# Layer two's third row block in halves of 256, and another order of the work list, in a two-layer transformer kernel

## The chip, the cores and the metric

The kernel runs on one core of a Trainium2 chip. The metric is the device time of one execution in microseconds (us). The profile is that of one further execution, taken by the hardware profiler; its span, from the first to the last instruction, is 1654.3 us.

## What is computed

An input x of 2048 rows and 512 columns (bf16) goes through attention, a two-product MLP, and both again with the same weights. Attention has 32 heads of width 16.

```python
def _A_ref(x, wqkv, wo):
    qkv = (x @ wqkv).reshape(B, S, 3, H, Dh).transpose(2, 0, 3, 1, 4)
    q, k, v = qkv[0], qkv[1], qkv[2]
    scores = jnp.einsum("bhqd,bhkd->bhqk", q, k) * (Dh ** -0.5)
    p = _softmax(scores, axis=-1)
    o = jnp.einsum("bhqk,bhkd->bhqd", p, v)
    return o.transpose(0, 2, 1, 3).reshape(B, S, D) @ wo
def _B_ref(x, w1, w2):          # w1 is 512 x 1792, w2 is 1792 x 512
    return jnp.maximum(x @ w1, 0) @ w2
x = x + _A_ref(_layernorm(x), wqkv, wo)
x = x + _B_ref(_layernorm(x), w1, w2)
x = x + _A_ref(_layernorm(x), wqkv, wo)
x = x + _B_ref(_layernorm(x), w1, w2)
```

## The kernel before

**Row blocks.** The queries of each layer are worked off in chunks (`chunks`, L440): (layer, number) gives the first tile of 128 rows and the number of tiles. Layer one has four chunks of 512 rows. Layer two has three of 512 and two of 256, the last 512 rows in halves.

**The loop.** A planner in Python writes one long program (the `while units:` loop, L1140 and on, to L1280 or so). Its unit is a score block: one head, 128 keys, 512 queries (or two key blocks of 256 queries in a half). Each turn of the loop banks three units in one of two PSUM tiles ps_s (score matmuls of TensorE, L1240, four heads lying in four groups of 32 rows of the array), and ScalarE takes the exponential of all three, or of two (L1249, 1536 or 1024 columns). Where it is two, VectorE computes the third block's exponential in bit arithmetic (lin L970, step L1010, cube L1018 to L1022). TensorE then multiplies the exponentials by the values into ps_o (L876). When a segment (four heads, all keys) is through, the sums are copied to u (L800, or L798 with an earlier part added), the denominators go by DMA to c and back (SP queue, L805 and L825), are spread over 32 partitions by a DMA of POOL's queue (L827) or by a shuffle on VectorE (L837), and multiplied into ot (L813). There are three buffers u, c and r. TensorE may repeat a score matmul where it would be idle.

**The work list.** Everything else is done beside this: q, k and v, the output product with wo and its addition to x (`o_group`, L630), the norm and its transposes (`ln_rows`, `ln_groups`, L550), the first MLP product with its relu (`h_group`, L664; w1 is fetched tile by tile through four buffers, L644) and the second (`z_group`, L690, with the store of the rows in layer two, L693). They stand in a list `work`. Each turn of the loop takes from it, from the front, the first group whose inputs the plan has as ready, as far as a pace allows that is set by what is left and how many turns remain. When all heads of a chunk are through, `rest_of_chunk` gives that chunk's groups, which are added at the end of the list. `before(l, j)` names the earlier chunk whose use of the shared tiles xn2T and ht has to be over.

**The end.** After the last exponential, `run_all` works off what the list still holds, with relus on ScalarE (L662). Then the last 256 rows follow in an order written out by hand: output product (L1303, with `add`), norm, MLP. Into this the second MLP products of the two tiles before (1536 to 1791) are woven: tile one under the norm (`half_part(0, ...)`), tile two one product a step in the MLP loop (`half_part(1, [ft])`).

Of the kernel before, what the change touches and what calls it, by code (L numbers as in the profile page):

```python
# [24 lines left out]
def kernel(  # L25
# [199 lines left out]

    slot = [0]
    now_pe = [0.0]
    now_dve = [0.0]  # L230
    mode = [None]
# [206 lines left out]


    chunks = {(l, j): (j * TPC, TPC) for l in range(2) for j in range(NQS)}  # L440
    chunks[1, NQS - 1] = (NKB - TPC, TPC // 2)
    chunks[1, NQS] = (NKB - TPC // 2, TPC // 2)

    def columns(l, j):

# [72 lines left out]
    def ln_rows(tag, tt, n, i):  # L518

        if tag not in ln_seq:  # L520
            ln_seq.append(tag)
        at_tag = ln_seq.index(tag)
        prev = ln_seq[at_tag - 1]
        old = [("xn", ln_seq[at_tag - 2], k) for k in range(TPC)] if at_tag > 1 else []
        if ("st", tag, i) not in made:
            task(830, lambda: ln_stats(tag, tt + i, i), [("st", tag, i)], old)
        if i == n - 1:

            def rstd():
                ln_rstd(tag, 0)  # L530
                ln_newton(tag)
                mark(("rs", tag, 3), lag=RSTD_LAG)

            task(500, rstd, [("rs", tag, 3)], each(n, "st", tag) + old)
            for k in range(n):
                task(
                    325, lambda k=k: ln_apply(tag, tt + k, k), [("xn", tag, k)],
                    [("xT", prev, k), ("rs", tag, 3)],
                )

    def ln_groups(tag, dst, at_column, n, war):
# [83 lines left out]
    def o_group(l, j, i):  # L625
        tt, n = chunks[l, j]
        a = columns(l, j)[1] + i * P

        def fin(b):
            nc.vector.tensor_add(out=x_t[tt + i][:], in0=x_t[tt + i][:], in1=b)  # L630
            mark(("o", l, j, i))
            ln_rows(("ln2", l, j), tt, n, i)

        return mm_group(
            [(ot[t][:, a : a + P], wo[:, t // 2, :]) for t in range(NT)], fin,
            [("o", l, j, i)],
            [("ot", l, j, t, i) for t in range(NT)],
        )
# [64 lines left out]
    def before(l, j):  # L703

        if (l, j) == (0, 0):
            return None
        return (l, min(j, NQS - 1) - 1) if j else (0, NQS - 1)

    def rest_of_chunk(l, j):

        b = before(l, j)
        xj, a, w = columns(l, j)
        n = w // P
        war_h = each(chunks[b][1], "z", *b) if b else []
        war_x = each(NF, "h", *b) if b else []
        gs = [o_group(l, j, i) for i in range(n)]
        gs += ln_groups(("ln2", l, j), xn2T, a, n, war_x)
        gs += [h_group(l, j, ft, war_h) for ft in range(0, NF, QS // w)]
        if (l, j) != (1, NQS - 1):
            gs += [z_group(l, j, i) for i in range(n)]  # L720
        if l == 0:
            gs += ln_groups(("ln1", 1, j), xnT[j], 0, TPC, [])
            gs.append(k_group(1, 0, j))
            gs += [v_group(1, kb) for kb in range(j * TPC, (j + 1) * TPC)]
            gs += [k_group(1, T, j) for T in range(1, 4)]
        return gs
# [20 lines left out]
    for l in range(2):  # L747


        if l == 0:  # L750
            steps = [(0, range(4), 0, TPC), (0, range(MID), TPC, 2 * TPC)]
            steps += [(0, range(MID), 2 * TPC, NKB), (0, range(MID, 4), TPC, NKB)]
            steps += [(j, range(4), 0, NKB) for j in range(1, NQS)]
        else:
            steps = [(0, range(4), 0, NKB - TPC), (1, range(NEXT), 0, NKB - TPC)]
            steps += [(0, range(4), NKB - TPC, NKB), (1, range(NEXT, 4), 0, NKB)]
            steps += [(1, range(NEXT), NKB - TPC, NKB)]
            steps += [(j, range(4), 0, NKB) for j in range(2, NQS + 1)]
        for j, Ts, a, b in steps:
            for T in Ts:  # L760
                sums = acc[8 * j :] if l else acc0
                add_run(l, j, T, range(a, b), load=a and sums, store=b < NKB and sums)
# [7 lines left out]
    def finish_segment(sg, last):  # L770
        l, j, t, e = sg["l"], sg["j"], sg["t"], sg["e"]
        sums_wait[0] += 1
        if sg["store"] is not None:

            def store():
                if sg["load"] is not None:
                    nc.vector.tensor_add(out=sg["store"], in0=sg["load"], in1=ps_o[:])
                else:
                    nc.vector.tensor_copy(out=sg["store"], in_=ps_o[:])
                mark(("po",))  # L780
                sums_wait[0] -= 1

            musts.append((EVAC, now_pe[0] + PE_TO_DVE, store))
            return
        n = norm_no[0]
        norm_no[0] += 1
        if n >= NU:
            run_until(("m", n - NU))
        u, r, c = ubuf[n % NU], rbuf[n % NU], cbuf[n % NU]
        lane = DH if e == 0 else DH - 1  # L790
        width = sg["w"]
        at_column = columns(l, j)[1]
        sums = u[lane : P : 32, 0:width]
        c = c[:, 0 : width // 32]

        def copy():
            if sg["load"] is not None:
                nc.vector.tensor_add(out=u[:], in0=sg["load"], in1=ps_o[:])  # L798
            else:
                nc.vector.tensor_copy(out=u[:, 0:width], in_=ps_o[:, 0:width])  # L800
            mark(("po",))
            mark(("u", n))
            sums_wait[0] -= 1
            if sg not in segs[-2:]:
                nc.sync.dma_start(out=c, in_=sums)  # L805
                mark(("c", n), lag=C_LAG)

        musts.append((77 + 1.045 * width, now_pe[0] + PE_TO_DVE, copy))
        b = before(l, j)
        war = each(chunks[b][1], "o", *b) if b else []  # L810

        def mul(a, w):
            nc.vector.scalar_tensor_tensor(  # L813
                out=ot[t][:, at_column + a : at_column + a + w], in0=u[:, a : a + w], scalar=mask[e][:, 0:1],
                in1=r[:, a : a + w], op0=ALU.mult, op1=ALU.mult,
            )
            for i in range(a // P, (a + w) // P):
                mark(("ot", l, j, t, i))

        ended[l, j] = ended.get((l, j), 0) + 1  # L820
        quick = sg["load"] is not None or ended[l, j] == NT

        def recip():
            nc.vector.reciprocal(out=c, in_=c)
            nc.sync.dma_start(out=sums, in_=c)  # L825
            if not quick:
                nc.gpsimd.dma_start(  # L827
                    out=r[:, 0:width],
                    in_=bass.AP(
                        tensor=sums.tensor, offset=sums.offset,  # L830
                        ap=[list(sums.ap[0]), [0, 32], [1, width]],
                    ),
                )
            mark(("r", n), lag=U_LAG if quick else R_LAG)

        def spread():
            nc.vector.stream_shuffle(  # L837
                out=r[:, 0:width], in_=u[:, 0:width], mask=[lane] * 32
            )

        def spread_mul():
            if quick:
                spread()
            mul(0, width)

        def direct(i):
            if i == 0:
                spread()
            a = i * P
            nc.vector.reciprocal(out=r[:, a : a + P], in_=r[:, a : a + P])  # L850
            mul(a, P)

        def direct_all():
            for i in range(width // P):
                direct(i)

        ots = each(width // P, "ot", l, j, t)
        if last:
            last_steps.append(direct)
        elif sg is segs[-2]:  # L860
            task(3100, direct_all, ots + [("m", n)], war + [("u", n)])
        else:
            task(165, recip, [("r", n)], [("c", n)], place=0)
            cost = 105 + 1.1 * width + (200 + 1.05 * width if quick else 0)
            task(cost, spread_mul, ots + [("m", n)], [("r", n)] + war)
        if ended[l, j] == NT and not last:
            work.extend(rest_of_chunk(l, j))

    pend = deque()
    musts = []  # L870
# [269 lines left out]
    while units:  # L1140
# [67 lines left out]
        if first["l"] and first["early"]:  # L1208
            rest = sum(x[0][0]["early"] for x in itertools.islice(units, 400)) / W - 20.0
        pace = (  # L1210
            3.0 if first["short"] and not first["l"] else max(todo / max(rest + (0.0 if first["j"] == NQS - 1 and not first["l"] else AHEAD[first["l"]] if first["j"] < NQS - 1 else -6.0), 6.0), 0.5)
        )
        owed[0] = min(owed[0] + pace, 6.0) if todo else 0.0
        hurry[0] = pace > (
# [67 lines left out]
    run_all()  # L1282
    ending[0], wide[0] = False, True
    users.clear()
    l, j = 1, NQS
    tag = ("ln2", l, j)
    tt, n_rows = chunks[l, j]
    rows = range(n_rows)
# [58 lines left out]
    for ft in range(NF + 1):  # L1347
# [17 lines left out]
        if ft:  # L1365
            for i in rows:
# [1 line left out]
                    banks[i], ht[ft - 1][:, part(i)], w2[:, ft - 1, :],  # L1368
                    False, ft == NF, "h",
                )  # L1370
        if ft < NF:
            half_part(1, [ft])
    for i in rows:
        copy = nc.vector.tensor_copy if i % 2 else nc.scalar.copy
        uses(copy(out=x_t[tt + i][:], in_=at_bank(banks[i])), banks[i])
# [33 lines left out]
```

The softmax here doesn't subtract the row's maximum and nothing guards it: scores larger than these inputs give would overflow.

## Time and profile before

| | |
|---|---|
| three executions | 1643.58, 1649.41, 1651.98 us; median 1649.41 |
| the profiled execution | 1656.09 us, span 1654.3 us |
| busy: TensorE, VectorE, ScalarE | 1509.3, 1507.4, 1590.0 us |
| mean granted TensorE clock | 0.981 |
| exponentials on ScalarE | 749 of 1536 columns at 1593 ns, 616 of 1024 at 1166 ns, one of 512 |
| score matmuls (L1240) | 4396 of 512 columns, 1164 of 256 |
| w1 tiles fetched (L644 and at the start) | 126 of 128 KB |

How to read it: PE is TensorE's matmuls, PEld its weight loads, DVE is VectorE, ACT is ScalarE, POOL is GpSimd, SPq the queue that issues DMAs. A row of the page's groups names line, engine, operation, output and inputs, then busy time, mean length in ns, and the idle time of the engine ahead of these instructions with what ended it. Idle time counts where the engine is the one that everything waits for. Matmuls that lie in different row groups of the array overlap, so their lengths don't add up to time.

### The profile page before, as it was taken

The page shows a single profiled execution, that of the slowest core. Times are in us where ns is not written, and L with a number is a line of the kernel's source. Part 1 is how long each engine was busy: PE and PEld are TensorE (multiplying, and loading weights), DVE is VectorE, ACT ScalarE, POOL GpSimd, SP SyncE. Part 2 cuts the span into 40 slices and gives each one's busy share as a digit, 9 for nine tenths or more (in the row PEclk, how much of TensorE's full clock was granted, in tenths as well). Part 3 has the DMA queues.
Part 4 walks back from the last instruction along what each step waited for, and adds up shares of the span by engine and source line. Part 5 has one row for each costly group of instructions (what it writes and reads, how often), then busy time and mean ns, then how long its engine had stood idle before and what let it go on. Part 6 is the DMA issues. An engine that isn't in the chain of part 4 may idle for free.

```text
span 1654.3 us, 32685 instructions
## 1 busy us (share of the span) xinstructions
PE 1509.3 (91%) x13512; PEld 493.4 (30%) x13512; DVE 1507.4 (91%) x3102; ACT 1590.0 (96%) x1393; POOL 86.7 (5%) x260
## 2 busy tenths in 40 slices
PE   8998889999989999999999998899999899999987
PEld 3222222222222222222222222223222222333334
DVE  7359999999999999899899998799999999999992
ACT  7999999999999999899999999999999999999982
POOL 2000001001010010100100000001000100010010
PEclk9999999999999999799999999899999999989999
DMA  5000000110002000021000100001200021001103
GB/s 160 1 1 2 2 2 15 40 27 15 2 17 47 20 13 8 11 46 24 9 1 17 30 1 1 2 3 23 45 16 21 13 48 27 16 18 35 33 16 89
DMA packets 104260, 37.92 MB, mean 23 GB/s; under 512 B 93712, under 2 KB 101648, under 8 KB 104112
## 3 DMA queue, kind: packets, MB, share of 16 engines
q1 hardware_dynamic: 92192, 24.38, 6.4%
q0 software_dynamic: 10576, 10.16, 3.2%
q8 instruction: 105, 1.72, 0.4%
q10 hardware_dynamic: 1344, 1.31, 0.2%
q14 instruction: 43, 0.35, 0.1%
HBM read 22.54 MB, written 2.10 MB: 15 GB/s over the span
## 4 chain that ended last, share of the span: by engine, by line
ACT 83%; PE 10%; DVE 5%; issue 1%; DMA 0%; POOL 0%; POOLq 0%; ACTq 0%; DVEq 0%
ACT e L1249 83%; PE ps_s L1240 3%; PE ps_o L876 3%; PE ps_f L430 2%; DVE lin L970 1%; PE ps_s L1303 1%; DVE stats L459 0%; DVE step L1010 0%; PE ps_f L510 0%; DVE cube L1018 0%; DMA w<-in_B_w_dram 0%; PE ps_s L430 0%; DVE cube L1019 0%; DVE cube L1022 0%; PE ps_f L1303 0%
## 5 line engine op out<-in xcount | busy, mean ns | idle before, releaser
L1249 ACT ACTIVATE e<-ps_s 128x1536 bf16<-128x1536 f32 (+1 forms) x1366 | 1575.4, 1400 | 14.5 <-PE ps_s L1240 13.9
L1240 PE MATMUL ps_s<-q,ktp 32*128 32x512 bf16 (+1 forms) x5560 | 610.6, 365 | 102.3 <-ACT e L1249 87.5
L876 PE MATMUL ps_o<-e,vaug 128*32 128x512 bf16 (+1 forms) x3906 | 523.5, 370 | 9.0 <-DVE u L800 3.1
L970 DVE TENSOR_SCALAR lin<-ps_s 128x512 int16<-128x512 f32 x616 | 419.8, 684 | 29.0 <-PE ps_s L1240 24.3
L1240 PEld LDWEIGHTS <-ktp 32*128 32x128 bf16 x5560 | 185.7, 92 | 527.5 <-issue 402.3
L876 PEld LDWEIGHTS <-vaug 128*32 128x32 bf16 x6012 | 157.8, 94 | 358.5 <-issue 346.3
L1010 DVE TENSOR_SCALAR step<-lin 128x1024 int16<-128x1024 int16 x616 | 242.5, 417 | 0.4
L1018 DVE TENSOR_TENSOR cube<-step 128x1024 f16<-128x1024 bf16 x308 | 209.2, 681 | 1.8 <-PE ps_o L876 0.2
L1022 DVE TENSOR_TENSOR cube<-cube,lin 128x1024 bf16<-128x1024 f16 x308 | 208.5, 677 | 0.0
L876 PE MATMUL ps_o<-cube,vaug 128*32 128x512 bf16 (+1 forms) x702 | 150.5, 363 | 0.0
L876 PE MATMUL ps_o<-step,vaug 128*32 128x512 bf16 (+1 forms) x702 | 145.8, 363 | 0.0
L876 PE MATMUL ps_o<-lin,vaug 128*32 128x512 bf16 (+1 forms) x702 | 129.5, 361 | 6.0 <-DVE u L800 3.8
L1019 DVE TENSOR_SCALAR cube<-cube 128x1024 f16<-128x1024 f16 x308 | 127.4, 415 | 1.3
L430 PE MATMUL ps_f<-xn2T,w 128*128 128x512 bf16 (+1 forms) x408 | 122.8, 384 | 3.3 <-DVE ht L664 1.3
L430 PE MATMUL ps_f<-w,ht 128*128 128x512 bf16 x392 | 121.0, 384 | 1.2 <-DVE q L607 0.5
L827 POOL DMA_DIRECT2D r<-u x45 | 32.6, 725 | 1202.9 <-DVE lin L970 590.4
L430 PE MATMUL ps_f<-xnT,wqkv 128*128 128x512 bf16 (+1 forms) x312 | 91.2, 376 | 3.9 <-DVE x L690 0.9
L607 DVE TENSOR_SCALAR q<-ps_f,qmask 128x512 bf16<-128x512 f32 (+1 forms) x94 | 63.4, 697 | 14.2 <-PE ps_f L430 13.9
L430 PE MATMUL ps_f<-wo,ot 128*128 128x512 bf16 x240 | 73.9, 384 | 1.2 <-DVE x L630 0.8
L664 DVE TENSOR_SCALAR ht<-ps_f 128x512 bf16<-128x512 f32 x98 | 67.1, 684 | 1.4 <-PE ps_f L430 0.9
L459 DVE BATCH_NORM_STATS2 stats<-x 128x6 f32<-128x512 bf16 x64 | 43.7, 683 | 16.2 <-ACT x L1313 14.1
L430 PEld LDWEIGHTS <-w 128*128 128x128 bf16 x448 | 35.5, 100 | 66.0 <-issue 49.6
(93 smaller groups left out, 607.0 us busy)
## 6 DMA issues: line engine op xcount, KB each, us to landing
w<-in_B_w_dram SPq DMA_DIRECT2D x126, 128.0 KB
r<-u POOLq DMA_DIRECT2D x32, 256.0 KB, 7.1
out_dram<-x SPq DMA_DIRECT2D x16, 128.0 KB
x<-in_A_x_dram SPq DMA_DIRECT2D x14, 128.0 KB
w<-in_B_w_dram SPq DMA_DIRECT2D x1, 1792.0 KB
r<-u POOLq DMA_DIRECT2D x13, 128.0 KB, 4.5
wqkv<-in_A_wqkv_dram ACTq DMA_DIRECT2D x2, 512.0 KB
c<-u SPq DMA_DIRECT2D x56, 8.0 KB
```

Source lines behind the costliest of these rows:

```text
L430: nc.tensor.matmul(out, lhsT, rhs, start=i % k == 0, stop=i % k == k - 1)
L459: nc.vector.bn_stats(out=st[:], in_=x_t[tt][:])
L607: return nc.vector.tensor_scalar(out=qbuf[n % 2][e][:, 0:w], in0=b, scalar1=qmask[e][:, 0:1], scalar2=None, op0=ALU.mult,)
L664: nc.vector.tensor_scalar(out=out, in0=sums, scalar1=0.0, scalar2=None, op0=ALU.max)
L876: nc.tensor.matmul(ps_o[32 * g : 32 * g + 32, 0 : sg["w"]], vaug[sg["l"]][kb][:, 4 * sg["T"] + g, 2 * e : 2 * e + 32], rhs, start=g not in ...
L970: first = nc.vector.tensor_scalar(out=lin[which][:, half * QS : (half + 1) * QS], in0=src, scalar1=EXP_BIAS, scalar2=0.0, op0=ALU.add, op1 ...
L1010: nc.vector.tensor_scalar(out=stair, in0=line, scalar1=keep, scalar2=put, op0=ALU.bitwise_and, op1=ALU.bitwise_or,)
L1018: (609, lambda: nc.vector.tensor_mul(out=power, in0=mantissa, in1=mantissa)),
L1019: (342, lambda: nc.vector.tensor_scalar(out=power, in0=power, scalar1=CUBE, scalar2=None, op0=ALU.mult)),
L1022: (609, lambda: nc.vector.tensor_mul(out=power.bitcast(BF16), in0=power, in1=line.bitcast(BF16))),
L1240: nc.tensor.matmul(b[:, a : a + sg["w"]], kt[32 * g : 32 * g + 32, kc : kc + P], qbuf[sg["n"] % 2][sg["e"]][32 * g : 32 * g + 32, 0 : sg[" ...
L1249: ex = nc.scalar.activation(out=eb[:, 0 : place[m]], in_=b[:, 0 : place[m]], func=ACTF.Exp, scale=1.0 / (LOG2E * UNIT),)
```

## The change

Layer two's chunks become two of 512 rows and four of 256: rows 1024 to 1535 are split as the last 512 already were. `LAST` is the number of the last chunk, 5. `before` gives the latest earlier chunk that shares the columns of xn2T and ht, and the norm's dependencies count the tiles of the chunks they refer to.

`rest_of_chunk` puts a chunk's output products and its norm's transposes at the front of the list, in both layers; the MLP goes to the end as before. Of the last chunk but one, the second MLP product of tile two is now a group of the list; the product of tile one stays in the hand-written end, and the line that wove tile two's into the final MLP loop is gone.

```diff
-    chunks[1, NQS - 1] = (NKB - TPC, TPC // 2)
-    chunks[1, NQS] = (NKB - TPC // 2, TPC // 2)
+    HALF = TPC // 2
+    for n in range(4):
+        chunks[1, 2 + n] = (2 * TPC + n * HALF, HALF)
+    LAST = 5
...
-        old = [("xn", ln_seq[at_tag - 2], k) for k in range(TPC)] if at_tag > 1 else []
+        rows_of_prev = chunks[prev[1:]][1]
+        before_that = ln_seq[at_tag - 2] if at_tag > 1 else None
+        old = each(chunks[before_that[1:]][1], "xn", before_that) if at_tag > 1 else []
...
-        return (l, min(j, NQS - 1) - 1) if j else (0, NQS - 1)
+        if not j:
+            return 0, NQS - 1
+        rows = chunks[l, j][0] % TPC
+        return max(
+            (l, b) for b in range(j)
+            if chunks[l, b][1] == TPC or chunks[l, b][0] % TPC == rows
+        )
...
-        gs += ln_groups(("ln2", l, j), xn2T, a, n, war_x)
-        gs += [h_group(l, j, ft, war_h) for ft in range(0, NF, QS // w)]
-        if (l, j) != (1, NQS - 1):
-            gs += [z_group(l, j, i) for i in range(n)]
+        work[0:0] = [o_group(l, j, i) for i in range(n)] + ln_groups(
+            ("ln2", l, j), xn2T, a, n, war_x
+        )
+        gs = [h_group(l, j, ft, war_h) for ft in range(0, NF, QS // w)]
+        gs += [z_group(l, j, i) for i in range((l, j) == (1, LAST - 1), n)]
...
-            steps += [(j, range(4), 0, NKB) for j in range(2, NQS + 1)]
+            steps += [(j, range(4), 0, NKB) for j in range(2, LAST + 1)]
...
-    l, j = 1, NQS
+    l, j = 1, LAST
...
-        if ft < NF:
-            half_part(1, [ft])
```

The pace's test for a chunk that is not the last one compares with `LAST` in layer two, where it compared with `NQS - 1`.

More of the change, by code (lines that the diff above doesn't have):

```diff
@@ L224, in uses @@
         log.append((ins.ins, w, makes))
-    slot = [0]
     now_pe = [0.0]
@@ L537, in ln_rows @@
                     325, lambda k=k: ln_apply(tag, tt + k, k), [("xn", tag, k)],
-                    [("xT", prev, k), ("rs", tag, 3)],
+                    [("xT", prev, k)] * (k < rows_of_prev) + [("rs", tag, 3)],
                 )
@@ L715, in rest_of_chunk @@
         war_x = each(NF, "h", *b) if b else []
-        gs = [o_group(l, j, i) for i in range(n)]
-        gs += ln_groups(("ln2", l, j), xn2T, a, n, war_x)
-        gs += [h_group(l, j, ft, war_h) for ft in range(0, NF, QS // w)]
-        if (l, j) != (1, NQS - 1):
-            gs += [z_group(l, j, i) for i in range(n)]
+        work[0:0] = [o_group(l, j, i) for i in range(n)] + ln_groups(
[3 more added lines that the diff above has]
+        gs += [z_group(l, j, i) for i in range((l, j) == (1, LAST - 1), n)]
         if l == 0:
@@ L866, in finish_segment @@
         if ended[l, j] == NT and not last:
-            work.extend(rest_of_chunk(l, j))
+            later = rest_of_chunk(l, j)
+            work.extend(later)
     pend = deque()
@@ L1210 @@
         pace = (
-            3.0 if first["short"] and not first["l"] else max(todo / max(rest + (0.0 if first["j"] == NQS - 1 and not first["l"] else AHEAD[first["l"]] if first["j"] < NQS - 1 else -6.0), 6.0), 0.5)
+            3.0 if first["short"] and not first["l"] else max(todo / max(rest + (0.0 if first["j"] == NQS - 1 and not first["l"] else AHEAD[first["l"]] if first["j"] < (LAST if first["l"] else NQS - 1) else -6.0), 6.0), 0.5)
         )
```

## The prediction

> **What bounds the kernel now.** I read the page's busy times first, then its chain of waits, then busy time by stretch, and last the end of the timeline instruction by instruction.
>
> ```profile
> span 1654.3 us, 32685 instructions
> PE 1509.3 (91%) x13512; PEld 493.4 (30%) x13512; DVE 1507.4 (91%) x3102; ACT 1590.0 (96%) x1393; POOL 86.7 (5%) x260
> ...
> ACT  7999999999999999899999999999999999999982
> ...
> PEclk9999999999999999799999999899999999989999
> ...
> ACT 83%; PE 10%; DVE 5%; issue 1%; DMA 0%; POOL 0%; POOLq 0%; ACTq 0%; DVEq 0%
> ...
> L1249 ACT ACTIVATE e<-ps_s 128x1536 bf16<-128x1536 f32 (+1 forms) x1366 | 1575.4, 1400 | 14.5 <-PE ps_s L1240 13.9
> ```
>
> ScalarE, with 1366 exponentials, is the chain: it idles 14.5 us ahead of all of them together. The row of tenths says where it isn't the bound: the first and the last slice (41.4 us each). So two things can be worth time: fewer or better fed exponentials, or a shorter end.
>
> In the same page PEclk dips in three slices. Finer stretches show the granted clock at 0.50 in bursts (682 to 697 us is one), and nearly all waits of the exponentials lie in or beside such bursts. The stretches that matter here (columns: length, then busy us of PE, PEld, DVE, ACT, POOL with counts, granted clock, DMA share, GB/s):
>
> ```profile
> 1215.00:1411.00 196.00, 182.25 (x1538) 57.13 (x1535) 192.44 (x389) 195.97 (x176) 8.99 (x19) 1.00 0.11 25
> ...
> 1490.00:1590.00 100.00, 94.36 (x1414) 37.59 (x1406) 97.62 (x206) 100.00 (x90) 5.09 (x7) 1.00 0.15 32
> ```
>
> The first stretch is rows 1024 to 1535 in one piece of 512, the second the last 512 rows, which already run in halves. ScalarE is at 100% in both, with 1.114 and 1.111 us per exponential: halves do not slow the loop while the clock is whole.
>
> The end of the timeline (start, length, instruction, wait before it):
>
> ```profile
> 1594.60 11.46 ACT L1249 ACTIVATE e<-ps_s 128x1536 bf16<-128x1536 f32 x9
> ...
> 1613.51 0.60 ACT L662 ACTIVATE ht<-ps_s 128x512 bf16<-128x512 f32 x1 [7.45 <-PE ps_s L430]
> ...
> 1623.51 0.60 ACT L662 ACTIVATE ht<-ps_s 128x512 bf16<-128x512 f32 x1 [1.43 <-PE ps_s L430]
> 1624.16 0.38 PE L1303 MATMUL ps_s<-x,ident 128*128 128x512 bf16 x1 [0.68 <-ACT ht L662]
> ...
> 1628.64 0.69 DVE L459 BATCH_NORM_STATS2 stats<-x 128x6 f32<-128x512 bf16 x1 [14.10 <-ACT x L1313]
> ...
> 1634.56 0.60 PE L1303 MATMUL ps_s<-xn2T,w 128*128 128x256 bf16 x4 [0.17 <-DVE xn2T L1344]
> ...
> 1650.16 0.69 DVE L1375 CAST x<-ps_s 128x512 bf16<-128x512 f32 x1 [1.74 <-PE ps_s L1303]
> ```
>
> The last exponential ends at 1594.60 + 11.46 = 1606.06. Then 48.24 us follow without any: norm and first MLP product of rows 1536 to 1791 (to 1624.16, 18.10), the output product of the last 256 rows (to 1628.64, 4.48), their norm (to 1634.56, 5.92), their MLP (to 1650.16, 15.60), the store (4.14).
>
> **What the Trainium skill says.** "TensorE: Matmul & The Clock Gate", section "Wait — 56ns, not 53.3ns?": back to back matmuls start N ÷ 2.4 GHz + 2.5 ns apart when warm, 215.7 ns at 512. The trace agrees: a step of the final MLP takes 1.085 us for four of 256 and three of 512, and 4 x 109.2 + 3 x 215.8 = 1084. Same page, "What's actually happening": the clock has two states, half and full, set by how busy windows of about 3.4 us were. The trace shows 0.50 and 1.00 and mixtures where a stretch holds both. Same page, Part 3, "The mechanism": weight loads overlap running matmuls of other row groups. The trace agrees so far as the half stretch has 29% more PEld time per us (37.59/100 against 57.13/196) at full ScalarE. "ScalarE: Activation LUTs", "Specifications": 1.2 GHz. The two exponential forms, 1593 and 1166 ns, differ by 427 ns for 512 columns, 0.83 ns each, as that clock gives.
>
> **The change part by part.** Counts come from the order of the built programs, durations from the rows.
>
> *Exponentials.* 1366 before and after; 753 of 1536 and 612 of 1024 columns instead of 749 and 616. At the second layer's rates (1571 and 1147 ns) this is 4 x 0.424 = +1.7 us on the path, the only term of the loop that surely is.
>
> *Rows 1024 to 1535 in halves.* Score matmuls: 587 fewer of 512, 1080 more of 256; by busy time per instruction (74.5/607 = 0.123, 73.7/1124 = 0.066) 71 more against 72 less. Those on ScalarE's exponentials: 876 x 0.076 against 434 x 0.153, even; on VectorE's the same kind of exchange. VectorE: 16 more copies u, mask products and q of 256 for 8 fewer of 512 each, +1.2, +1.7, +1.7; 21 relus of two 256 for 14 of 512, +4.8; 16 short reciprocals for 8, +1.1; two fewer pairs of its own exponentials, -7.9: about +4 us with the small ones, over 1590 us in which it has some 100 us free. Nothing on the path; the 100% of the half stretch is the reason. The SP queue gets 14 more loads of 128 KB (weights of the first product read twice) and 8 more pairs of c and u transfers, POOL 7 more row spreads and 12 small operations. Behind the weight loads in SP's queue stand c and u transfers, and behind those the product into ot and the reuse of three u buffers. A half lasts some 11 exponentials (12 us), three buffers 36 us; the last 512 rows lived with that without a wait of ScalarE outside a clock dip. Nothing taken, 0 to 2 us kept.
>
> *Order of the work list.* Output products and transposes now go ahead of older MLP work, in both layers: the products for rows 512 to 1023 stand at exponential 361 instead of 364, those of 1024 at 532 instead of 548, in layer two 1049 instead of 1069. Same instructions, other places, hidden by the same exponentials. At exponential 1023 a normalisation now stands directly before the u copy that needs its buffer, with eight matmul pieces finished ahead: 8 x 0.216 = 1.7 us at most, taken as 0. The other unknown is how often PE runs thin enough for the clock to halve. Before, this cost 13.9 us; bounds -13.9 (none left) and +8 (two more bursts of 4), taken as 0.
>
> *The end.* In the new order rows 1536 to 1791 have output product at exponential 1309, norm at 1320, all relus by 1352 and one of the two second products at 1362. No work is left between the last exponential and the last rows' output product. (a) The first such matmul waits for the last ps_o product alone, which ends at 1606.83: 18.10 becomes 0.8. (b) Its 16 early matmuls take 3.45, to E + 4.25 (E: end of the exponentials). Beside them VectorE does copy u 0.42, shuffle 0.44, then twice reciprocal 0.95 and product 0.35, from E + 0.81 to about E + 4.4; row two's last product needs that at E + 4.65, before its cast. 4.48 stays. (c) The norm stays, 5.92, with the 15 matmuls of the first row block under it as now. (d) The MLP loses 14 matmuls of 512, 14 x 0.216 = 3.0: 12.6. A step is then 0.868; its relu (0.2 wait, 0.42, 0.2 back) fits in the 0.87 until its sums are needed. The w1 loads: in the stretch 1614 to 1623, where PE waits for them, a buffer was used again after 3.72, 3.57, 3.35, 3.13, 3.04 and 3.45, mean 3.38; the new pace asks for 4 x 0.868 = 3.47, so only the 0.25 and 0.10 above it wait: +0.3. (e) Store 4.14.
>
> Sum of the end: 0.8 + 4.48 + 5.92 + 12.9 + 4.14 = 28.2 against 48.2: -20.0. With +1.7 the span is 1654.3 - 18.3 = 1636.0. The profiled execution took 1656.1, the three timed ones 1643.6 to 1652.0 with median 1649.4; the same difference there gives **1631.1 us**, 1.1% faster.
>
> **The rivals.**
> *Thin PE, half clock* (0.20): the burst that before lay at 1610 to 1617 moves onto the output product of the end (PE was busy 1.85 of the 3 us to 1606, then 0.83 of 3): 16 matmuls at half speed, +3.5, and the new order has one or two bursts more in the loop, +4 to +8. For it: bursts follow stretches with 2 of 3 us busy. Against: the output product now follows at once. Gain halved: about 1640, range 1638 to 1650.
> *Fewer bursts* (0.10): more real work in the last 400 us keeps the clock up; up to 10 of the 13.9 us come back: 1621.
> *PE takes over the pace in rows 1024 to 1535* (0.05, slower): double matmul counts over 176 exponentials. It turns the sign at 18.3 us, 0.10 per exponential, and gives over 0.5% from 26.5 us, 0.15 each; at 0.16 each 1631 + 28 = 1659. For it: in the dip 1460 to 1479 the half stage lost 3.1 us of ScalarE. Against: 1.111 us per exponential at whole clock.
> *The work doesn't fit and spills behind the loop after all* (0.02): about 1649. The order speaks against it.
>
> **How the numbers follow.** The forecast has 0.63 (1624 to 1638). A measurement tells 0.5%, 8.2 us, from no change: faster is below 1641.2. Faster: 0.63 + 0.10 + half of the 0.20 = 0.83; within: 0.10 + 0.02 = 0.12; slower 0.05. The range 1620 to 1643 holds the forecast, nearly all of the second rival and half of the first.
>
> **What would show it.** Right: exponentials still 100% in the half stretches; no L662 rows on ACT; the first output product under 1 us after the last product into ps_o; steps of 0.87; about 28 us after the last exponential. Wrong: waits of L1249 above 20 us, PEclk at 0.5 behind the last exponential, or PE waiting for w in the final steps.

## The result and the profile after

| | before | after |
|---|---|---|
| median of four executions | 1650.54 us | 1626.82 us |
| lowest and highest | 1643.58, 1651.98 | 1625.63, 1627.23 |
| span of the profiled execution | 1654.3 | 1625.4 |
| end of the last exponential in it | 1606.06 | 1597.00 |
| from there to the end | 48.24 | 28.40 |
| idle ahead of the exponentials | 14.5 | 5.9 |
| mean TensorE clock in it | 0.981 | 0.997 |

The ratio of the times is 0.9863, with an interval of 0.9834 to 0.9892. The forecast was 1631.1, in a range of 1620 to 1643. So sign and size were right; how the gain is made up was only half right.

The page of the kernel after: busy times, the row of ScalarE's tenths, the granted clock, the chain of waits, and the group of the exponentials (busy, mean ns, idle before).

```profile
span 1625.4 us, 35105 instructions
PE 1453.3 (89%) x14536; PEld 505.4 (31%) x14728; DVE 1508.8 (93%) x3133; ACT 1584.7 (97%) x1385; POOL 95.8 (6%) x279
...
ACT  6999999999999999999999999999999999999994
...
PEclk9999999999999999999999998999999999999999
...
ACT 83%; DVE 9%; PE 6%; issue 2%; DMA 0%; ACTq 0%; DVEq 0%
...
L1259 ACT ACTIVATE e<-ps_s 128x1536 bf16<-128x1536 f32 (+1 forms) x1366 | 1574.8, 1408 | 5.9 <-PE ps_s L1250 5.6
```

ScalarE is still the chain. Its last slice is at four tenths instead of two: that is the shorter end. Of the three slices in which the clock dipped one is left. And the exponentials' idle time fell by 8.6 us, which the prediction had taken as unchanged.

Busy time by stretch, after (columns as in the prediction): rows 1024 to 1535 in halves, then the last 512 rows.

```profile
1215.00:1390.00 175.00, 159.39 (x2395) 65.21 (x2419) 170.01 (x368) 175.00 (x154) 16.72 (x37) 1.00 0.13 27
1490.00:1590.00 100.00, 91.62 (x1433) 41.89 (x1441) 97.42 (x213) 100.00 (x88) 8.35 (x19) 1.00 0.22 46
```

Both have ScalarE at 100% and the clock at 1.00; VectorE and TensorE are idle for 3 to 9% of the time. The halves do not slow the loop.

The end of the timeline, after (start, length, instruction, wait before it):

```profile
1579.60 17.40 ACT L1259 ACTIVATE e<-ps_s 128x1536 bf16<-128x1536 f32 x14
...
1597.71 1.67 PE L1313 MATMUL ps_s<-wo,ot 128*128 128x512 bf16 x7 [0.16 <-issue]
...
1601.98 0.69 DVE L460 BATCH_NORM_STATS2 stats<-x 128x6 f32<-128x512 bf16 x1 [0.86 <-ACT x L1323]
...
1607.90 1.03 PE L1313 MATMUL ps_s<-xn2T,w 128*128 128x256 bf16 x8 [0.18 <-DVE xn2T L1354]
...
1614.75 0.33 PEld L1313 LDWEIGHTS <-w 128*128 128x128 bf16 x4 [0.34 <-DMA w<-in_B_w_dram]
...
1616.45 0.33 PEld L1313 LDWEIGHTS <-w 128*128 128x128 bf16 x4 [1.16 <-DMA w<-in_B_w_dram]
1616.46 0.61 PE L1313 MATMUL ps_s<-xn2T,w 128*128 128x256 bf16 x4 [0.66 <-DMA w<-in_B_w_dram]
...
1621.66 0.69 DVE L1383 CAST x<-ps_s 128x512 bf16<-128x512 f32 x1 [1.52 <-PE ps_s L1313]
```

The exponentials end at 1579.60 + 17.40 = 1597.00, and the output product follows at once: no relu stands between. The steps of the MLP are 0.868 apart. Two loads of weights wait for w; the first wait (0.34) does not hold its step up, after the second (1.16) the step begins at 1616.46, 1.71 after the one before, so 0.84 late.

### The profile page after: what moved, and what is told of

Its sections match the earlier page's. It is cut to its first block, busy times and chain, and to the rows that moved or that the text cites. A ratio compares the mean times of both kernels' runs of the same rounds, so it can differ in the third digit from the quotient of the medians.

```text
span 1625.4 us, 35105 instructions
## 1 busy us (share of the span) xinstructions
PE 1453.3 (89%) x14536; PEld 505.4 (31%) x14728; DVE 1508.8 (93%) x3133; ACT 1584.7 (97%) x1385; POOL 95.8 (6%) x279
## 4 chain that ended last, share of the span: by engine, by line
ACT 83%; DVE 9%; PE 6%; issue 2%; DMA 0%; ACTq 0%; DVEq 0%
ACT e L1259 83%; DVE lin L980 2%; PE ps_s L1250 2%; PE ps_f L429 1%; PE ps_o L886 1%; DVE step L1020 1%; DVE cube L1032 1%; DVE cube L1028 1%; PE ps_s L1313 1%; DVE cube L1029 1%; DVE ht L667 0%; DVE q L610 0%; DVE stats L460 0%; DVE ot L822 0%; DVE u L809 0%
## 5 line engine op out<-in xcount | busy, mean ns | idle before, releaser
L1259 ACT ACTIVATE e<-ps_s 128x1536 bf16<-128x1536 f32 (+1 forms) x1366 | 1574.8, 1408 | 5.9 <-PE ps_s L1250 5.6
L1250 PE MATMUL ps_s<-q,ktp 32*128 32x512 bf16 (+1 forms) x6053 | 599.6, 341 | 111.8 <-ACT e L1259 92.3
L886 PE MATMUL ps_o<-e,vaug 128*32 128x512 bf16 (+1 forms) x4348 | 513.0, 345 | 16.1 <-DVE u L809 5.9
L980 DVE TENSOR_SCALAR lin<-ps_s 128x512 int16<-128x512 f32 x612 | 418.0, 687 | 23.7 <-PE ps_s L1250 19.0
L886 PEld LDWEIGHTS <-vaug 128*32 128x32 bf16 x6664 | 166.6, 94 | 345.8 <-issue 334.8
L886 PE MATMUL ps_o<-cube,vaug 128*32 128x512 bf16 (+1 forms) x772 | 146.5, 341 | 0.4 <-issue 0.3
L429 PE MATMUL ps_f<-w,ht 128*128 128x512 bf16 x348 | 108.8, 384 | 5.1 <-issue 3.8
L836 POOL DMA_DIRECT2D r<-u x52 | 38.1, 732 | 1188.3 <-DVE lin L980 603.6
L429 PE MATMUL ps_f<-xnT,wqkv 128*128 128x512 bf16 (+1 forms) x287 | 81.8, 361 | 4.4 <-issue 1.1
L610 DVE TENSOR_SCALAR q<-ps_f,qmask 128x512 bf16<-128x512 f32 (+1 forms) x102 | 65.0, 660 | 10.1 <-PE ps_f L429 7.9
L667 DVE TENSOR_SCALAR ht<-ps_f 128x512 bf16<-128x512 f32 x105 | 72.2, 687 | 2.1 <-PE ps_f L429 1.2
L429 PE MATMUL ps_f<-wo,ot 128*128 128x512 bf16 x207 | 66.0, 384 | 4.5 <-issue 2.4
L822 DVE SCALAR_TENSOR_TENSOR ot<-u,mask,r 128x512 bf16<-128x512 f32 (+2 forms) x82 | 51.2, 626 | 1.1
```

What stands on the lines that cost most here:

```text
L429: nc.tensor.matmul(out, lhsT, rhs, start=i % k == 0, stop=i % k == k - 1)
L610: return nc.vector.tensor_scalar(out=qbuf[n % 2][e][:, 0:w], in0=b, scalar1=qmask[e][:, 0:1], scalar2=None, op0=ALU.mult,)
L667: nc.vector.tensor_scalar(out=out, in0=sums, scalar1=0.0, scalar2=None, op0=ALU.max)
L822: nc.vector.scalar_tensor_tensor(out=ot[t][:, at_column + a : at_column + a + w], in0=u[:, a : a + w], scalar=mask[e][:, 0:1], in1=r[:, a ...
L886: nc.tensor.matmul(ps_o[32 * g : 32 * g + 32, 0 : sg["w"]], vaug[sg["l"]][kb][:, 4 * sg["T"] + g, 2 * e : 2 * e + 32], rhs, start=g not in ...
L980: first = nc.vector.tensor_scalar(out=lin[which][:, half * QS : (half + 1) * QS], in0=src, scalar1=EXP_BIAS, scalar2=0.0, op0=ALU.add, op1 ...
```

## The experiments

Each is the kernel after with one part taken back, or the kernel before with one part added, except for the last three; the diffs are all against the kernel after. "Tail" is the time from the end of the last exponential to the end of the span, in the profiled execution. "At full clock" is a straight line through the executions' times against their mean granted clocks, read at clock 1.0; with four executions it is rough (some 2 us), with twenty it is good to about 1.5 us, and for the kernel without repeats, whose clocks lie far from 1.0, only to some 4 us. Ratios are to executions of before on the same chip; their median was 1650.54 for after, 1649.83 for the four kernels below it, 1652.37 for the layer-one order and the three last kernels, 1651.82 for the one without halves.

The end of the exponentials, the waits and the tail are those of one execution each, and these differ in clock: before was profiled below its mean (0.981 against 0.986), halves alone and the kernel without repeats above theirs (0.995 against 0.987, 0.961 against 0.953). The tails can be compared; the ends of the exponentials and the waits only where the clocks are close.

| | median us | ratio to before, interval | exponentials' end | waits | tail | mean clock of the executions | at full clock |
|---|---|---|---|---|---|---|---|
| before (23 executions) | 1649.83 | | 1606.06 | 14.5 | 48.2 | 0.9864 | 1637.0 |
| after | 1626.82 | 0.9863, 0.9834 to 0.9892 | 1597.00 | 5.9 | 28.4 | 0.9962 | 1625.2 |
| halves alone | 1651.50 | 1.0009, 0.9992 to 1.0026 | 1603.17 | 11.6 | 38.1 | 0.9869 | 1638.4 |
| order alone | 1629.31 | 0.9881, 0.9847 to 0.9915 | 1592.28 | 3.6 | 32.7 | 0.9965 | 1626.3 |
| without the moved product | 1628.78 | 0.9880, 0.9848 to 0.9913 | 1595.99 | 5.9 | 30.7 | 0.9960 | 1625.6 |
| order in layer two only | 1633.29 | 0.9907, 0.9873 to 0.9941 | 1599.24 | 7.2 | 29.9 | 0.9900 | 1625.2 |
| order in layer one only | 1638.29 | 0.9926, 0.9908 to 0.9944 | 1596.06 | 6.7 | 39.6 | 0.9918 | 1632.1 |
| order and moved product, no halves | 1630.61 | 0.9889, 0.9831 to 0.9948 | 1593.48 | 4.7 | 34.0 | 0.9945 | 1626.4 |
| no repeated score matmuls | 1655.45 | 1.0011, 0.9994 to 1.0027 | 1615.24 | 20.7 | 30.1 | 0.9530 | 1618.6 |
| six w1 buffers | 1625.52 | 0.9844, 0.9827 to 0.9860 | 1597.18 | 5.9 | 27.5 | 0.9975 | 1623.3 |
| six w1 buffers, more repeats | 1630.44 | 0.9877, 0.9854 to 0.9900 | 1601.54 | 9.7 | 29.4 | 0.9958 | 1625.7 |

### Halves alone

The output products and transposes stand at the end of the list as before, and tile two's second product stays in the final loop; layer two's rows 1024 to 1535 are in halves.

```diff
-        work[0:0] = [o_group(l, j, i) for i in range(n)] + ln_groups(
+        gs = [o_group(l, j, i) for i in range(n)] + ln_groups(
             ("ln2", l, j), xn2T, a, n, war_x
         )
-        gs = [h_group(l, j, ft, war_h) for ft in range(0, NF, QS // w)]
-        gs += [z_group(l, j, i) for i in range((l, j) == (1, LAST - 1), n)]
+        gs += [h_group(l, j, ft, war_h) for ft in range(0, NF, QS // w)]
+        if (l, j) != (1, LAST - 1):
+            gs += [z_group(l, j, i) for i in range(n)]
...
+        if ft < NF:
+            half_part(1, [ft])
```

> Rows 1024 to 1535 in halves, but output products and transposes stay at the end of the list and tile two's second product stays in the final MLP loop. In its order five relus (L662's kind, on ScalarE) are still behind the last exponential, and at exponential 1071 four output products are forced in one go, since the halves' ot needs them (4 x 8 x 0.216 = 6.9 us of TensorE ahead of the scores). My theory (the two parts need each other): end 0.5 + 5 x 1.8 + 4.5 + 5.9 + 15.6 + 4.1 = 39.6 us (before 48.2, after 28.4), a wait of the exponentials of 5 to 9 us near exponential 1071; time 1640 to 1652. Rival (the halves alone bring the gain, the order of the list is idle): end 31 us, no such wait, time under 1634.

Measured: no gain, 1.0009, as the theory had it. The tail is 10.1 us shorter, and the medians at nearly the same mean clock (0.9869 and 0.9864) are equal, so the loop must have become longer by about as much. The two profiles can't show this directly, because their clocks differ (0.995 and 0.981). What this kernel's profile does show is one wait of 6.8 us at full clock; the mix of exponentials, 753 and 612 as in after, adds 1.7 by the prediction's price, and the rest of the 10 us is not placed. The timeline at the wait:

```profile
1256.24 1.89 PE L429 MATMUL ps_f<-wo,ot 128*128 128x512 bf16 x7 [0.28 <-DVE q L610]
...
1258.90 1.89 PE L429 MATMUL ps_f<-wo,ot 128*128 128x512 bf16 x8 [0.78 <-DVE x L633]
...
1261.57 1.89 PE L429 MATMUL ps_f<-wo,ot 128*128 128x512 bf16 x8 [0.78 <-DVE x L633]
...
1263.84 4.67 ACT L1260 ACTIVATE e<-ps_s 128x1024 bf16<-128x1024 f32 x4 [6.84 <-PE ps_s L1251]
```

Output products that had waited in the list behind older MLP work became due all at once, because the tiles of ot that they read were to be written again: three runs of matmuls in a row, each followed by VectorE's addition, and no score matmul in between. Right behind them, at 1264.10, stand the products into ot. With halves these buffers come round twice as often; with halves and the new order, in after and in the kernel without the moved product, no such wait is left, so the order of the list is what gets the products out in time.

### Order alone

No halves, the second product in the final loop; only the front of the list is new.

```diff
-    for n in range(4):
-        chunks[1, 2 + n] = (2 * TPC + n * HALF, HALF)
-    LAST = 5
+    for n in range(2):
+        chunks[1, 3 + n] = (3 * TPC + n * HALF, HALF)
+    LAST = 4
```

Tile two's product goes back as in the diff above.

> Only the order of the work list: rows 1024 to 1535 in one piece as before, tile two's second product in the final MLP loop as before. In its order two relus are left behind the last exponential instead of seven. My theory: end 0.5 + 2 x 1.8 + 4.5 + 5.9 + 15.6 + 4.1 = 34.2 us, 14 less than before; time 1633 to 1640. Rival (the order of the list is idle without halves): end 45 us or more, time 1645 or more.

Measured: 1629.31, below what was expected; this one part has nearly nine tenths of the gain (20.5 of 23 us against 1649.83). Its tail is 4.3 us longer than after's, but its loop ends 4.7 us earlier, with 3.6 us of waits and no burst of half clock between 640 and 720 us. Whether the halves and the moved product add anything to the whole time is therefore not settled: after's median is 2.5 us lower, but the intervals of the two ratios overlap, and the profiled executions, at clocks of 0.997 (after) and 0.999, took 1625.4 and 1625.0 us. Two relus still run behind the last exponential, which ends at 1592.28:

```profile
1594.21 0.60 ACT L665 ACTIVATE ht<-ps_f 128x512 bf16<-128x512 f32 x1 [1.92 <-PE ps_f L429]
1595.08 0.60 ACT L665 ACTIVATE ht<-ps_s 128x512 bf16<-128x512 f32 x1 [0.28 <-PE ps_s L429]
```

### Without the moved product

After, with tile two's second product in the final loop again.

```diff
-        gs += [z_group(l, j, i) for i in range((l, j) == (1, LAST - 1), n)]
+        if (l, j) != (1, LAST - 1):
+            gs += [z_group(l, j, i) for i in range(n)]
...
+        if ft < NF:
+            half_part(1, [ft])
```

> The changed kernel with tile two's second product back in the final MLP loop. My theory: 14 steps of 1.085 instead of 0.868 and no waits for w1 there (after had 1.5 us of them): end 30 to 31.5 us instead of 28.4, time 1628 to 1631. Rival (the steps are held by the w1 loads anyway): no change, end 28.4.

Measured: the tail is 2.3 us longer than after's, inside the expected 30 to 31.5. The 14 matmuls it carries in the final loop are 3.0 us; the shorter steps of the kernel after give some of it back to waits for w (below). The halves added to the order, then, cut 2.0 us from its tail (32.7 to 30.7) and end the loop 3.7 us later (1592.28 to 1595.99). The time, 1628.78, can't be told from after's: the intervals overlap.

### Order in one layer only

Two kernels: after with the new order in layer two only, and before with the new order in layer one only.

```diff
-        work[0:0] = [o_group(l, j, i) for i in range(n)] + ln_groups(
+        gs = [o_group(l, j, i) for i in range(n)] + ln_groups(
             ("ln2", l, j), xn2T, a, n, war_x
         )
-        gs = [h_group(l, j, ft, war_h) for ft in range(0, NF, QS // w)]
+        if l == 1:
+            work[0:0] = gs
+            gs = []
+        gs += [h_group(l, j, ft, war_h) for ft in range(0, NF, QS // w)]
...
```

(with `if l == 0` in the second, which has before's row blocks and final loop).

> The changed kernel with the new order of the list in layer two alone; layer one as before. End 28.4 us. It tells apart why the exponentials waited 5.6 us instead of 13.9. Theory A (the order in layer one keeps TensorE from running thin there): bursts of half clock return near 680 to 705 us with 4 to 6 us of waits, time 1631 to 1634. Theory B (the bursts come and go with the plan as a whole and with the execution): waits elsewhere or none, time 1624 to 1631.

> The kernel before with the new order of the list in layer one alone; halves, layer two's list and the final MLP loop as before. In its order six relus are left behind the last exponential. End 0.5 + 6 x 1.8 + 4.5 + 5.9 + 15.6 + 4.1 = 41.4 us, 6.8 less than before. Theory A (the old order empties the list while the norm of rows 1024 to 1535 of layer one is under way, TensorE runs thin and its clock halves near 680 us; older MLP work kept behind the norm prevents it): no burst between 640 and 720 us, waits of the exponentials 4 to 6 us less than before's 14.5 in total, mean clock higher, time 1636 to 1641. Rival B (bursts come and go with the execution, whatever the order of layer one): clock 0.986 as before's mean, time 1643 or more.

Both came out as the first theory has it, with waits a little off the expected sizes. With the order in layer two only, the burst of half clock near 680 us is back (3.7 us of waits, 4 to 6 expected), and the kernel loses 6.5 us to after; all four of its executions took longer than all of after's. With the order in layer one only it is gone (waits 7.8 less than before's, 4 to 6 less expected), and the kernel wins 14 us on before without the halves; its tail of 39.6 is still long. The profiles agree throughout: the burst is in all three with the old order in layer one (before, halves alone, layer two only), and in the eight with the new order the clock is 1.00 from 640 to 720 us. What the burst comes from can be read from the timeline of before, just ahead of it:

```profile
677.07 0.68 DVE L630 TENSOR_TENSOR x<-x,ps_f 128x512 bf16<-128x512 bf16 x1
...
680.50 0.20 POOL L492 TENSOR_TENSOR ta<-ya 128x4 f32<-128x4 f32 x1 [5.11 <-DVE ya L474]
...
681.13 0.61 PE L1240 MATMUL ps_s<-q,ktp 32*128 32x512 bf16 x6 [0.95 <-ACT e L1249]
```

At 677 us the last output product of a chunk is added to x. What the list holds after it hangs on that chunk's norm, whose Newton steps then run on GpSimd. Until the first transpose at 688.11 TensorE has only scores and values, and waits for exponentials. Busy time by stretch of before, ahead of the burst and in it:

```profile
677.00:682.00 5.00, 3.18 (x33) 1.01 (x30) 4.86 (x14) 5.00 (x6) 1.17 (x5) 0.99 0.21 43
682.00:697.00 15.00, 15.00 (x101) 3.80 (x97) 10.22 (x23) 11.65 (x9) 2.52 (x8) 0.50 0.01 2
```

The same view of after, where these steps run at 654.6 to 659.5 us, and the one burst that is left:

```profile
654.00:660.00 6.00, 5.31 (x47) 1.70 (x45) 5.77 (x15) 6.00 (x6) 4.40 (x12) 1.00 0.00 0
985.00:995.00 10.00, 9.64 (x54) 1.90 (x54) 7.71 (x16) 7.84 (x7) 1.49 (x4) 0.50 0.00 1
```

In before, TensorE was busy 3.18 of 5 us, and from 682 on the clock is half for 15 us, in which ScalarE works 11.65. After, it was busy 5.31 of 6 us, with products of xnT and wqkv from the list beside the norm, and the clock stays whole: since the newest chunk's output products run first, other work is left for the time of its norm. The one burst that is left, at 985 us, follows 2.66 busy of 4 us, at the switch of layers, where the norm's steps again run with nothing of the list beside them.

That the order in layer one decides on the burst at 680 us is shown by these two kernels; that it does so through the work left beside the norm is read from the timelines. A thin stretch does not bring a burst every time, though. In the order alone TensorE was as thin at the switch of layers (2.27 us busy of the 3.4 from 981.7, against 2.25 from 981.4 in after), and the clock stayed whole. The same holds for after at 1060 us, near the place of before's burst at 1057:

```profile
1060.00:1065.00 5.00, 3.33 (x34) 1.11 (x29) 4.96 (x12) 5.00 (x5) 0.00 (x0) 1.00 0.04 5
```

So of the other bursts that went (60, 1055 to 1083, 1460 us), that the change took them away is not shown; those near 60 and 1060 us are no matter of this order alone (one stands at 65 us in the kernel with six buffers and more repeats, one at 1055 in the order in layer two only, none there in halves alone).

### Order and moved product without halves

```diff
-    for n in range(4):
-        chunks[1, 2 + n] = (2 * TPC + n * HALF, HALF)
-    LAST = 5
+    for n in range(2):
+        chunks[1, 3 + n] = (3 * TPC + n * HALF, HALF)
+    LAST = 4
```

> The kernel after, with rows 1024 to 1535 in one piece of 512 again: the new list order and tile two's second MLP product in the list stay. Theory (the halves make the room): without them two relus and that product still stand behind the last exponential, so the product's 3.0 us come ahead of the output product instead of in the MLP loop. About 2 us of the MLP loop are saved and 3 to 3.5 us come in front: tail 33 to 35 us, against 32.7 with the order alone and 28.4 with all parts; time 1628 to 1632. Rival (the moved product gains its 2.3 us without halves): tail 30 to 31 us, time 1625 to 1628.

Measured: 1630.61, tail 34.0, as the theory had it. The moved product doesn't fit in the loop, and it stands ahead of the first output product (timeline of this kernel, whose last exponential ends at 1593.48):

```profile
1596.29 2.97 PE L429 MATMUL ps_s<-w,ht 128*128 128x512 bf16 x13
...
1600.10 0.38 PE L1313 MATMUL ps_s<-x,ident 128*128 128x512 bf16 x1 [0.85 <-DVE x L693]
```

So the moved product pays in the tail only together with the halves: with them it takes 2.3 us off (30.7 to 28.4), without them it adds 1.3 (32.7 to 34.0). The halves bring the chunk's work forward far enough that the product is done under the exponentials. In the whole time the difference to after lies within the intervals.

### How much the clock is worth, and the loads of w1

The kernel after without the repeated score matmuls (921 fewer weight loads on PEld; their results are overwritten in any case, so the output is the same).

```diff
-    FLOOR = 0.56
+    FLOOR = 0.0
```

> The changed kernel without repeated score matmuls (a setting of the plan at 0 instead of 0.56): 4096 x 512 columns of score matmuls instead of 4931, so TensorE has 17% less of them. The repeats' products are overwritten, so nothing else changes but the plan. If thin TensorE work is what halves the clock: mean clock under 0.95, waits of the exponentials above 40 us, time above 1660. Rival (the repeats don't matter for the clock, and only fill TensorE): clock 0.995 and more, time 1622 to 1628.

Measured: 28.6 us slower than after by the medians, some 24 by the ratios to before. The direction is right, the size is not: mean clock 0.953 instead of below 0.95, a median of 1655 instead of over 1660, and 20.7 us of waits instead of over 40, these in an execution with a clock of 0.961. Its page:

```profile
span 1645.3 us, 33470 instructions
...
PEclk9999679999999999999999999879999999999999
...
L1259 ACT ACTIVATE e<-ps_s 128x1536 bf16<-128x1536 f32 (+1 forms) x1366 | 1578.4, 1426 | 20.7 <-PE ps_s L1250 17.3
```

In some of its stretches at half clock ScalarE doesn't wait at all (180 to 185 and 210 to 215 us: clock 0.50, ScalarE busy for all 5 us); so a burst need not cost anything while TensorE's work fits at half clock.

Six w1 buffers instead of four, alone and with more repeats (`FLOOR = 0.60`, 179 more weight loads on PEld):

```diff
-    NW1 = 4
+    NW1 = 6
```

> The changed kernel with six buffers for w1 instead of four. In the final MLP a buffer then has 6 x 0.868 = 5.2 us from one use to the next instead of 3.47. If the 1.5 us in which the changed kernel's final MLP waits for w1 are the four buffers: no such wait, end 26.9 instead of 28.4 us, time 1624.5 to 1626. Rival (the loads wait for each other in the queue, not for a buffer): the waits stay, time 1626 to 1628.

> Six buffers for w1, and the plan's setting for repeated score matmuls at 0.60 instead of 0.56: 5079 x 512 columns instead of 4931. In its order no work is left behind the last exponential. If the remaining 5.6 us of waits are bursts of half clock by thin TensorE: clock 0.998 or more, waits under 3 us, time 1621 to 1624.5. Rival (more repeats only delay other work and the scores): waits 6 us or more, time 1625 to 1632.

Measured with six buffers: 1625.52, the fastest of all, and a tail of 27.5. No load of weights waits for w in it any more; the MLP's first matmul and its last cast:

```profile
1608.09 1.03 PE L1313 MATMUL ps_s<-xn2T,w 128*128 128x256 bf16 x8 [0.18 <-DVE xn2T L1354]
...
1620.99 0.69 DVE L1383 CAST x<-ps_s 128x512 bf16<-128x512 f32 x1 [1.52 <-PE ps_s L1313]
```

That is 12.90 us, where after has 1621.66 - 1607.90 = 13.76: the waits for w cost 0.86, less than the 1.5 us for which the loads of weights waited. The medians differ by 1.3 us, and the intervals of the ratios overlap. More repeats don't help: the tail is 1.9 us longer than with six buffers alone, with the clock at 0.51 from 1601.5 to 1605 us, and the exponentials wait 9.7 us, 4.9 of it in one place near 1200 us.

## Why the prediction was right, and where it wasn't

**The end.** Predicted 28.2 us, measured 28.40, with errors that cancel. To the norm's first statistics 1601.98 - 1597.00 = 4.98 (0.8 + 4.48 predicted); the norm 5.92, as predicted; the MLP 13.76 (12.9); the last cast to the end 1625.4 - 1621.66 = 3.74 (4.14). Of the 0.86 by which the MLP was longer, 0.56 are the loads of w1, taken as +0.3 and worth 0.86 by the run with six buffers; the other 0.30 are the MLP without waits, 12.90 there instead of 12.6. The mean of six turnarounds, 3.38 us, was set against a pace of 3.47, though single ones took up to 3.72; a queue without slack pays for the late ones and isn't paid back for the early ones.

**The exponentials' mix.** Predicted +1.7; their busy time fell by 0.6. The term itself is sound: the order alone has 747 and 618 exponentials of the two forms, after has 753 and 612, which gives 6 x 0.424 = 2.5, and their busy times differ by 1574.8 - 1572.1 = 2.7. What it left out is most likely that exponentials also get busier in bursts. The kernel without repeats speaks for it: 14.8 us more waits than after and 3.6 us more busy time, although its mix should make it 0.8 less, so 0.30 us for each of waiting. For the burst waits that went here that makes about 3 us less, where 2.3 are to be explained.

**Clock bursts.** Taken as 0, between -13.9 and +8. This is the step that failed. The waits fell by 8.6, although the forced product below adds 2.0, so the bursts give about -10.6, and with the busy time some -13 us in this pair of profiles. The pair overstates it, since before was profiled below its mean clock; the line below gives -9 to -11 for the medians. The second rival (fewer bursts, "more real work in the last 400 us") had the right sign and the wrong place: the largest single part is at 680 us, in layer one, where the prediction had noted the order's new places (exponential 532 instead of 548) and not asked what TensorE would have beside the norm. What the runs showed in place of the 0 is that this order keeps TensorE busy there and the clock whole.

**The forced product.** "1.7 us at most, taken as 0." It costs 2.0 us of waits in two pieces. The timeline of after:

```profile
1199.36 1.90 PE L429 MATMUL ps_f<-w,ht 128*128 128x512 bf16 x8
...
1201.64 1.94 ACT L1259 ACTIVATE e<-ps_s 128x1024 bf16<-128x1024 f32 x2 [1.12 <-PE ps_s L1250]
...
1203.42 0.40 PE L886 MATMUL ps_o<-e,vaug 128*32 128x512 bf16 x4 [1.41 <-DVE u L807]
...
1204.46 2.37 ACT L1259 ACTIVATE e<-ps_s 128x1536 bf16<-128x1536 f32 x2 [0.88 <-PE ps_s L1250]
```

The eight matmuls run in one piece ahead of the scores (1.12), and then the copy u comes late and holds back the value products and the next scores (0.88). The bound counted only the first.

**The sum.** Forecast 18.3 us less; measured 28.9 less in the two profiles and 23.7 less in the medians of four. The line through before's 23 executions separates the two kinds: 0.97 us for each 0.001 of mean clock, and 1637.0 at full clock. With the same slope, after would be near 1623.1 at full clock (1626.82 less 3.8 x 0.97), an estimate; the line through its own four executions, whose clocks differ by only 0.002, gives 1625.2. So some 12 to 14 us of the gain against 1649.83 are work that went off the path, and 9 to 11 us go with the clock (0.9864 to 0.9962). The forecast had 18.3 and 0. That the total came within 5 us of it is partly luck: the work gave less than forecast, and the clock, of which nothing was forecast, gave the difference and more. The work's part is less than the sum of the end, -20, the mix, +1.7, and the forced product, +2.0, would make it; a part of before's tail lay at half clock too (0.53 from 1610 to 1617 us), and the line counts that as clock. How much of the rest is the line's own error stays open.

**The rivals.** "Thin PE, half clock" behind the last exponential is out: the clock is 1.00 from 1597 to 1622. "PE takes over the pace" is out: 100% of ScalarE in both stretches. "Spills behind the loop" is out for the whole change; two relus do spill with the order without halves, and the moved product as well where it is in the list. Of the signs named for being wrong one came, PE waiting for w in the final steps; it cost the 0.86 us.

## What to carry to other kernels

Where a list of side work fills an engine whose clock follows its load, the order of the list can matter more than how finely its work is cut: do first what the next chain of small steps hangs on, so that older independent work is left to run beside that chain. Before splitting work finer, ask which shared buffers come round sooner, and whether their readers stand in the list in time; here halves alone gained 10 us at the end and lost as much in the loop, 6.8 of it to one forced group. A load that must come back in almost exactly the time the consumer takes isn't hidden; its late arrivals are on the path.

## What the runs showed of the hardware that was not expected

The time of this kernel, which ScalarE bounds, follows TensorE's mean clock closely: over 23 executions of before, at 0.980 to 0.991, the times lie within 1.4 us (standard deviation) of a line of -0.97 us for each 0.001; halves alone, with 20 executions, gives -1.02. A mean clock lower by 0.001 is 3.3 us more at half clock, so 1 us at half clock costs about 0.3 us. It is no fixed price: between after and the kernel without repeats, which also has less work for TensorE, it is about 0.6 us for each 0.001 (24 to 29 us for 0.043). The span between lowest and highest of before (1644.1 to 1656.6) is thus mostly clock; after, at 0.995 to 0.997, lies within 1.6 us.

The Trainium skill, "TensorE: Matmul & The Clock Gate", section "What's actually happening", says the fall to half clock comes after an idle window of about 3.4 us. In before no such stretch of TensorE was idle ahead of the burst at 682: it was busy 3.18 of the 5 us, and 1.99 of the 3.4 us up to 682. So thin work can be enough for the fall. It is not always: in the kernel without repeats the clock stayed whole with TensorE less busy than that.

```profile
1110.00:1115.00 5.00, 3.08 (x32) 1.11 (x32) 4.96 (x12) 5.00 (x5) 0.00 (x0) 1.00 0.02 2
```

With 5.31 of 6 us the clock stayed whole too. No run here fixes a bound. The clock record of before agrees with a window of that length: its bursts lasted 6.8, 17.1, 10.2, 6.8, 13.7 and 6.8 us, whole multiples of 3.4.
